# One attention-and-feed-forward kernel: the denominator of the last batch by another route, and a new written order of work

## The chip, the cores and the metric

The kernel runs on one core of one Trainium2 chip. The metric is the device time of one execution in microseconds (us); lower is better. The core has five engines that this text names by their short names in the profile: PE (TensorE, the matrix engine; PEld is its weight load), DVE (VectorE), ACT (ScalarE), POOL (GpSimd) and SP (SyncE, which here only issues DMAs). SBUF is the on-chip working memory, PSUM the memory into which PE writes and from which DVE and ACT read.

## The reference

Four batches of four heads, 1088 positions, 32 features a head, in float32. Each query and key is projected to 8 numbers by S1 and to 8 by S2, and the 64 pairwise products are its features. Attention is linear in them; its output, 128 numbers a position, goes through a feed-forward layer of width 2048.

```python
def phi(x):
    a = np.einsum('rd,bhsd->bhsr', S1, x)
    b = np.einsum('rd,bhsd->bhsr', S2, x)
    return np.einsum('bhsi,bhsj->bhsij', a, b).reshape(*x.shape[:-1], r * r)
q_p, k_p = (phi(q), phi(k))
kv = np.einsum('bhsf,bhsd->bhfd', k_p, v)
z = np.sum(k_p, axis=2)
num = np.einsum('bhsf,bhfd->bhsd', q_p, kv)
den = np.einsum('bhsf,bhf->bhs', q_p, z)[..., None] + 1e-06
return (num / den).astype(np.float32)
...
h = x @ w_in
g = h * (1.0 / (1.0 + np.exp(-beta * h)))
return (g @ w_out).astype(np.float32)
```

## The kernel before, in words

**Two jobs woven together.** The feed-forward part is cut into 68 waves of 1024 columns of hidden values. The step `f17a`, `f17b` (function `first`, L725) is two matmuls of 512 columns that fill a two-bank PSUM tile `wave` for wave 17; one ACT instruction (L734, SiLU) then reads the whole tile into `gT`; `s17a`, `s17b` (function `second`, L757, or L749 for the last two chunks) multiply it by the output weights into `acc`. There are two `wave` tiles, so a new `f` needs the ACT instruction of the wave two before it. Eight waves make a chunk of 512 positions; the last three chunks have 256 positions and four waves each. Positions are packed over batches: 34 units of 32 positions a batch. Chunk 5 (waves 40 to 47) still needs batch 2 alone; chunk 6, from wave 48, is the first that needs batch 3.

**The attention steps of a batch b** (the batch is the last digit of a step's name): `kta`, `ktb`, `qt` transpose the loaded rows on DVE; `kpj`, `qpj` project on PE; `ktn`, `qtn` turn the result back on DVE; `kp0` to `kp3` form the key features (`k_product`, L372, on POOL or DVE); `kv0` to `kv3` sum features times v on PE (L520); `kvo` and three small DMAs `kr` spread that sum. The denominator takes a route of its own: `zs` (L393) lets PE sum products of the projections into z, `zc` copies it out, `wp` (L407) folds S2 into it, `wm` masks it, `cpj` (L450) multiplies the transposed queries by it, `ctn` turns the result, `c`, on DVE (L461). Then `dp` (L473) multiplies the first query projection with c, `ds` sums, `dr` takes the reciprocal (L490), `an` scales the projection by it (L496). `qp` forms the scaled query features (L372), `qpt` transposes them, `num` (L571) multiplies them with the spread sum on PE, and `xa`, `xb`, `xc` (`x_copy`, L601) copy the result to `xall`, in half precision, from where the waves read it. Batch 0 does its query side in two parts; the first has an `x` in its names.

**Copies of the last batch.** The last two chunks (16 units) leave the kernel in another layout, and `x_copy` writes those units of batch 3 in an interleaved order. So each of `xa3`, `xb3`, `xc3` is two instructions.

**What sets the order.** Nothing is scheduled automatically: `ORDER` is one list of step names, written out, and every engine's queue is that list filtered to its own instructions. Each engine runs its queue strictly in order, so one late step holds all behind it. `ENGINES` says on which engine the movable steps run. `i5` in the list is five matmuls on zeros that nobody reads (L340). SP issues all loads in the list's order too: `lk`, `lq`, `lv` for keys, queries and values, `li`, `lba`, `lo` for the weights, which `wb` (L310) and `wo` (L313) rescale. `wb0` and `wo0` serve waves 0 and 1, `wb1` and `wo1` waves 2 and 3, and so on. Keys and queries of batches 1 to 3 share one buffer, so `lk20` waits until `kta1` and `ktb1` have read batch 1.

```python
KC = ((0, 2), (2, 4), (4, 6), (6, 9))
XPARTS = (("x", (0, 4)), ("", (4, NC)))
...
for name in ORDER.split():
    if name[0] == "i" and name[1:].isdigit():
        idle(int(name[1:]))
    else:
        ops.pop(name)()
```

Of the kernel before, what the change touches and what calls it, by code (L numbers as in the profile page):

```python
# [12 lines left out]
P = 128  # L13
# [4 lines left out]
def kernel(  # L18
# [34 lines left out]
    lk0a ls2 lk0b lq0a ident pads warm i3 lv02 li0 lv00 ls1 lb i4 zms tbl lv01 sp kta0 masks ktb0 i2 sbd lv03  # L53
    qt0x0 kpj0 ktn0 sel kp10 sp2 kp30 bt i2 s2s lk11 lba1 li2 kp20 bc i3 kp00 zs0 lk10 zc0 qpjx0 wp0 wm0 i1 i2
    lba0 qtnx0 cpjx0 kv00 rb i5 ctnx0 kv30 kv10 kv20 kvw0 kvt0 dpx0 lo0 dsx0 drx0 anx0 qp00 lq0b li1 i7 kvc0 lo1
    qp10 qpt10 qpt00 lba3 lba2 ktb1 numx0 qt00 lq11 cpj0 lq10 xcx0 kta1 li3 qpj0 wb0 wo0 wb1 xax0 xbx0 wo1 i1
    f0a f0b ctn0 f1a qtn0 lo2 wb2 f1b lk21 dp0 lk20 ds0 kpj1 dr0 an0 f2a qp30 f2b s0a qp20 f3a f3b lv11 s0b s1a
    lo3 qt01 s1b s2a s2b lv13 qpt30 ktn1 qt11 wb3 f4a f4b f5a s3a qpt20 wo2 s3b f5b zs1 qpj1 qtn1 lv10 f6a zc1
    s4a wp1 wm1 f6b kp01 s4b wo3 num0 xb0 xc0 kta2 cpj1 xa0 lq20 f7a lq21 lv12 f7b kp21 s5a f8a kp31 s5b f8b
    ktb2 s6a ctn1 s6b s7a f9a kp11 f9b s7b lk30 f10a f10b kpj2 kv31 kv21 kv11 kv01 dp1 lk31 ds1 dr1 f11a f11b  # L60
    an1 qp21 o0 f12a s8a qt02 kvo1 f12b kr21 s8b kr31 ktn2 qp01 s9a s9b qpt21 qpt01 s10a f13a f13b s10b s11a
    qp11 qpt11 kr11 qt12 s11b f14a kp02 s12a f14b s12b f15a s13a lv23 s13b ktb3 f15b zs2 num1 zc2 lv21 s14a xc1
    s14b lq31 xa1 xb1 kp32 s15a lv20 lv22 s15b f16a f16b f17a kta3 wp2 f17b qpj2 wm2 cpj2 f18a f18b kp22 kp12
    qtn2 ctn2 f19a dp2 f19b lq30 kpj3 kv12 kv22 f20a o1 ds2 f20b dr2 s16a an2 f21a f21b kv02 qp02 kv32 f22a f22b
    s16b s17a f23a kvo2 f23b s17b s18a qpt02 s18b f24a f24b s19a kr22 s19b f25a qp12 f25b s20a s20b s21a lv30
    f26a f26b kr32 ktn3 qpt12 qp22 s21b s22a f27a f27b s22b s23a qpt22 s23b f28a f28b lv32 kr12 zs3 num2 zc3 xb2
    o2 wp3 xa2 f29a f29b xc2 lv31 s24a s24b kp33 f30a lv33 f30b s25a kp03 s25b qt13 s26a wm3 s26b f31a qt03 f31b
    s27a f32a f32b cpj3 qpj3 f33a f33b f34a s27b s28a f34b s28b s29a s29b f35a kp23 f35b s30a ctn3 s30b f36a
    qtn3 kp13 f36b dp3 ds3 s31a kv23 dr3 kv13 f37a f37b s31b o3 f38a an3 f38b kv03 qp13 kv33 f39a f39b kvo3 s32a
    s32b qp23 f40a kr23 f40b s33a s33b s34a f41a f41b kr13 qp03 s34b s35a f42a f42b s35b s36a s36b f43a kr33  # L70
    f43b s37a s37b qpt03 f44a f44b s38a qpt13 qpt23 s38b s39a f45a f45b s39b num3 xb3 o4 f46a f46b s40a xa3 xc3
    f47a f47b s40b s41a s41b f48a f48b s42a s42b f49a f49b s43a s43b f50a f50b s44a s44b s45a f51a f51b s45b
    s46a f52a f52b s46b s47a s47b f53a f53b f54a o5 f54b s48a s48b s49a f55a f55b s49b s50a f56a f56b s50b s51a
    f57a f57b s51b s52a s52b f58a f58b s53a s53b f59a f59b s54a s54b s55a s55b f60a f60b f61a o6 f61b s56a s56b
    s57a s57b f62a f62b s58a s58b f63a f63b s59a s59b o7 s60a f64a f64b s60b s61a f65a f65b s61b s62a s62b f66a
    f66b s63a s63b o8 f67a f67b s64a s64b s65a s65b s66a s66b s67a s67b o9
# [3 lines left out]
        "kp10": "p", "kp30": "p", "kp20": "p", "kp00": "v", "zc0": "a", "kvw0": "a", "qp00": "p", "kvc0": "a",  # L80
        "qp10": "v", "xcx0": "a", "wb0": "p", "wo0": "p", "wb1": "p", "xax0": "a", "xbx0": "a", "wo1": "p",
        "wb2": "p", "qp30": "v", "qp20": "p", "wb3": "p", "wo2": "p", "zc1": "a", "kp01": "p", "wo3": "p",
        "xb0": "a", "xc0": "a", "xa0": "a", "kp21": "p", "kp31": "p", "kp11": "p", "qp21": "p", "qp01": "p",
        "qp11": "p", "kp02": "p", "zc2": "a", "xc1": "v", "xa1": "a", "xb1": "a", "kp32": "p", "kp22": "p",
        "kp12": "v", "qp02": "v", "qp12": "v", "qp22": "p", "zc3": "v", "xb2": "a", "xa2": "v", "xc2": "v",
        "kp33": "p", "kp03": "p", "kp23": "v", "kp13": "v", "qp13": "p", "qp23": "p", "qp03": "v", "xb3": "a",
        "xa3": "v", "xc3": "v",
# [370 lines left out]
    def c_turn(b, c0, c1):  # L458
        if "tcc" not in st[b]:
            st[b]["tcc"] = sb.tile([P, G, R], F32, tag="tcc", name="tcc")  # L460
        nc.vector.transpose(  # L461
            out=ap(st[b]["tcc"], c0 * T, [[1, (c1 - c0) * T]]),
            in_=ap(c_at(b, c0), c0 * T, [[1, (c1 - c0) * T]]),
        )
# [6 lines left out]
    def den_product(b, c0, c1):  # L471
        g0, n = 4 * c0, 4 * (c1 - c0)
        nc.vector.tensor_tensor(  # L473
            out=prods[b % 2][:, g0 : g0 + n, 0:R],
            in0=ap(st[b]["tq"], g0 * 2 * R, [[2 * R, n], [1, R]]),
            in1=st[b]["tcc"][:, g0 : g0 + n, :],
            op=ALU.mult,
        )
# [8 lines left out]
    def den_turn_over(b, c0, c1):  # L487
        own(b, "rden", [P, G])
        g0, n = 4 * c0, 4 * (c1 - c0)
        nc.vector.reciprocal(out=st[b]["rden"][:, g0 : g0 + n], in_=st[b]["den"][:, g0 : g0 + n])  # L490

    def a_scale(b, c0, c1):
        own(b, "an", [P, G, R])
        g0, n = 4 * c0, 4 * (c1 - c0)
        a = ap(st[b]["tq"], g0 * 2 * R, [[2 * R, n], [1, R]])
        nc.vector.tensor_tensor(  # L496
            out=st[b]["an"][:, g0 : g0 + n, :], in0=a, in1=ap(st[b]["rden"], g0, [[1, n], [0, R]]), op=ALU.mult
        )
# [14 lines left out]
    def kv_sum(b, cs):  # L513
        kp = st[b]["kp"]
        t = kv_at(b)
        for c in cs:
            n = P if c < NC - 1 else 64
            done = st[b].setdefault("kvn", 0)
            for h in range(H):
                nc.tensor.matmul(  # L520
                    out=t[T * h : T * h + T, :],
                    lhsT=v_in[b][:n, h, c, :],
                    rhs=kp[:n, 4 * c + h, :],
                    start=(done == 0),
                    stop=(done == NC - 1),
                    skip_group_check=True,
                )
            st[b]["kvn"] += 1

# [49 lines left out]

    TURNED = 16  # L580

    def x_copy(b, j, c0, c1, eng):

        js, tile = ((0, 1), 0) if j < 0 else ((j,), j)
        n = min(c1, (U - js[0] + 3) // 4) - c0
        cut = n
        if b == B - 1:
            cut = min(n, (U - TURNED - js[0] + 3) // 4 - c0)
            assert all((U - TURNED - x + 3) // 4 - c0 == cut for x in js)
        for k0, k1 in ((0, cut), (cut, n)):  # L590
            if k0 == k1:
                continue
            u = 4 * (c0 + k0) + js[0]
            step_j, step_t = T, 1
            at = b * S + u * T
            if k0 == cut and b == B - 1:
                v = u - (U - TURNED)
                step_j, step_t = 1, 4
                at = b * S + (U - TURNED) * T + v // 4 * P + v % 4
                assert v % 4 + len(js) <= 4  # L600
            eng(  # L601
                out=ap(xall, at, [[step_j, len(js)], [P, k1 - k0], [step_t, T]]),
                in_=ap(st[b]["xp", c0][tile], k0 * T, [[512, len(js)], [T, k1 - k0], [1, T]]),
            )

    KC = ((0, 2), (2, 4), (4, 6), (6, 9))
    XPARTS = (("x", (0, 4)), ("", (4, NC)))
    for b in range(B):
# [4 lines left out]
        step(f"zs{b}", z_sum, b)  # L613
        step(f"zc{b}", lambda b=b: z_copy(b, cop(f"zc{b}")))
        step(f"wp{b}", w_project, b)
        step(f"wm{b}", w_mask, b)
# [13 lines left out]
        for x, us, (c0, c1) in parts:  # L630
            for i, (u0, u1) in enumerate(zip(us, us[1:])):
                step(f"qt{i}{x}{b}", q_transpose, b, u0, u1)
            step(f"qpj{x}{b}", q_project, b, c0, c1)
            step(f"qtn{x}{b}", q_turn, b, c0, c1)
            step(f"cpj{x}{b}", c_project, b, c0, c1)
            step(f"ctn{x}{b}", c_turn, b, c0, c1)
            step(f"dp{x}{b}", den_product, b, c0, c1)
            step(f"ds{x}{b}", den_sum, b, c0, c1)
            step(f"dr{x}{b}", den_turn_over, b, c0, c1)
            step(f"an{x}{b}", a_scale, b, c0, c1)  # L640
# [18 lines left out]
    assert u == B * U and TURNED == sum(n for _, n in chunks[-2:])  # L659
# [10 lines left out]
    turned = (LAST - 1, LAST)  # L670

# [43 lines left out]
    def first(s, w):  # L715
# [7 lines left out]
        for i in range(half):  # L723
# [4 lines left out]
                rhs=xall[:, u0 * T : u0 * T + n],  # L728
# [79 lines left out]
```

## Time and profile before

| | us |
|---|---|
| Median of 3 runs (lowest, highest) | 103.58 (103.08, 103.79) |
| The profiled execution, its own time | 103.39 |
| Its span, first to last instruction | 101.6 |
| Around the span | 1.8 |
| First wave matmul on PE (`f0a`) starts | 17.96 |
| `num3`, the last attention matmuls, start and next wave matmul | 72.95 and 74.45 |
| Last matmul ends | 97.74 |

| us busy of the span | PE | DVE | ACT | POOL |
|---|---|---|---|---|
| 0 to 18 | 16.2 | 11.1 | 4.0 | 12.0 |
| 18 to 72 | 53.9 | 43.3 | 44.8 | 28.6 |
| 72 to 96 | 23.2 | 4.6 | 22.3 | 0 |

Times in the profile are counted from the first instruction. A matmul's busy time overlaps that of its neighbours, since they are pipelined; what one costs PE is the distance from its start to the next one's start, and that is what is used below. The granted clock of TensorE was 1.00 over the span.

### The profile page before, as it was taken

What the parts mean: (1) busy time and instruction counts of PE and PEld (TensorE: products, weight loads), DVE (VectorE), ACT (ScalarE), POOL (GpSimd) and SP (SyncE); (2) the same over time, 40 slices, a digit from 0 to 9 for tenths busy, and PEclk for the clock granted to TensorE, in tenths of its full rate; (3) what the DMA queues carried; (4) which work ended last, traced back from release to release, by engine and by line L of the source; (5) the groups of instructions that cost most, each with busy time, mean ns of one, the idle gap of its engine ahead of it and who ended that gap; (6) DMA issues with size and microseconds to landing.
All of it is one profiled execution on the core that took longest, in us unless ns stands there. A gap on an engine that the chain in (4) does not pass through costs nothing.

```text
span 101.6 us, 3172 instructions
## 1 busy us (share of the span) xinstructions
PE 94.9 (93%) x1342; PEld 48.2 (47%) x1342; DVE 59.3 (58%) x111; ACT 72.5 (71%) x93; POOL 40.6 (40%) x49
## 2 busy tenths in 40 slices
PE   5999989999999999999999999999979999999940
PEld 1244554344436454344436434544424436689930
DVE  1564888999798994798953967389342020021110
ACT  1412022687795984789995779899967999989930
POOL 6409599999997993008090000085000000000000
PEclk9999999999999999999999999999999999999999
DMA  2999999983661545614320064052003205013411
GB/s 43 326 285 315 388 354 404 328 250 84 238 219 31 91 99 161 215 25 76 83 74 13 10 100 110 0 87 55 0 13 60 37 11 92 0 19 67 74 54 52
DMA packets 24253, 12.56 MB, mean 124 GB/s; under 512 B 17024, under 2 KB 21936, under 8 KB 24240
## 3 DMA queue, kind: packets, MB, share of 16 engines
q1 hardware_dynamic: 24032, 12.29, 43.8%
q8 instruction: 10, 0.16, 0.7%
q10 hardware_dynamic: 208, 0.08, 0.3%
q14 instruction: 3, 0.02, 0.1%
HBM read 9.84 MB, written 2.23 MB: 119 GB/s over the span
## 4 chain that ended last, share of the span: by engine, by line
PE 86%; ACT 8%; DVE 1%; issue 1%; DVEq 0%; ACTq 0%
PE wave L725 27%; PE acc L757 23%; PE idle L340 9%; ACT gT L734 7%; PE at L520 6%; PE xp L571 5%; PE fin L749 4%; PE qpp L430 3%; PE at L450 2%; PE kpp L357 2%; PE at L393 2%; PE xw L571 1%; PE at L548 1%; ACT xall L601 1%; PE at L407 1%
## 5 line engine op out<-in xcount | busy, mean ns | idle before, releaser
L734 ACT ACTIVATE gT<-wave 128x1024 f16<-128x1024 f32 (+1 forms) x69 | 65.8, 1011 | 8.3 <-PE wave L725 7.8
L725 PE MATMUL wave<-xall,winb 128*128 128x512 f16 (+1 forms) x160 | 40.8, 347 | 1.0 <-DVE xall L601 0.7
L757 PE MATMUL acc<-gT,woutp 128*128 128x512 f16 (+1 forms) x128 | 34.7, 366 | 0.0
L372 POOL TENSOR_TENSOR qp<-an,tq 128x768 f32<-128x768 f32 (+1 forms) x8 | 13.9, 1759 | 22.1 <-DVE an L496 22.1
L725 PEld LDWEIGHTS <-winb 128*128 128x128 f16 x160 | 14.7, 99 | 16.7 <-issue 3.8
L757 PEld LDWEIGHTS <-woutp 128*128 128x128 f16 x128 | 12.4, 97 | 12.8 <-issue 0.4
L372 POOL TENSOR_TENSOR kp<-tk 128x512 f32<-128x512 f32 (+1 forms) x12 | 15.0, 1274 | 6.3 <-DVE tk L368 6.3
L684 DVE STREAM_TRANSPOSE osb<-acc 128x512 f32<-128x512 f32 (+1 forms) x8 | 5.4, 680 | 18.0 <-PE acc L757 15.1
L508 DVE STREAM_TRANSPOSE qpt<-qp 128x768 f32<-128x768 f32 (+1 forms) x13 | 11.1, 883 | 0.3 <-POOL qp L372 0.2
L340 PE MATMUL idle<-warm 128*128 128x512 f16 x30 | 9.6, 454 | 1.3 <-DVE tiny L231 1.3
L344 DVE STREAM_TRANSPOSE kT<-k_in 128x576 f32<-128x576 f32 (+1 forms) x8 | 5.6, 715 | 2.4 <-DMA k_in<-in_k_dram 2.4
L571 PE MATMUL xp<-qpt,kvr 32*32 32x288 f32 (+2 forms) x160 | 6.9, 364 | 0.0
L571 PE MATMUL xw<-qpt,kvr 32*32 32x256 f32 (+1 forms) x160 | 6.8, 343 | 0.0
L520 PE MATMUL at<-kp,v_in 128*32 128x64 f32 (+1 forms) x288 | 6.3, 223 | 0.0
L520 PEld LDWEIGHTS at<-kp,v_in 128*32 128x32 f32 (+1 forms) x288 | 4.7, 109 | 3.2 <-issue 1.7
L349 DVE STREAM_TRANSPOSE qT<-q_in 128x512 f32<-128x512 f32 (+1 forms) x8 | 5.7, 718 | 0.3 <-DMA q_in<-in_q_dram 0.3
L310 POOL TENSOR_TENSOR winb<-w_in_sb,beta_all 128x512 f16<-128x512 f32 x4 | 5.2, 1292 | 0.0
L340 PEld LDWEIGHTS <-warm 128*128 128x128 f16 x30 | 2.9, 111 | 4.5 <-issue 1.6
L601 ACT CAST xall<-xw 128x128 f16<-128x128 f32 (+1 forms) x9 | 2.6, 327 | 3.0 <-PE xw L571 2.0
L571 PEld LDWEIGHTS xp<-qpt,kvr 32*32 32x32 f32 x160 | 3.7, 103 | 2.3 <-issue 0.8
L372 DVE TENSOR_TENSOR qp<-an,tq 128x768 f32<-128x768 f32 (+1 forms) x5 | 4.5, 905 | 0.1
L749 PE MATMUL fin<-woutp,gT 128*128 128x128 f16 x64 | 4.4, 219 | 0.0
(74 smaller groups left out, 71.1 us busy)
## 6 DMA issues: line engine op xcount, KB each, us to landing
k_in<-in_k_dram SPq DMA_DIRECT2D x6, 272.0 KB, 4.6
q_in<-in_q_dram SPq DMA_DIRECT2D x6, 272.0 KB, 4.0
v_in<-in_v_dram SPq DMA_DIRECT2D x8, 144.0 KB, 3.6
v_in<-in_v_dram SPq DMA_DIRECT2D x8, 128.0 KB, 3.3
w_in_sb<-in_moe_w_in_dram SPq DMA_DIRECT2D x4, 256.0 KB, 5.1
beta_all<-in_moe_beta_dram SPq DMA_DIRECT2D x4, 256.0 KB, 6.0
w_out_sb<-in_moe_w_out_dram SPq DMA_DIRECT2D x4, 256.0 KB, 5.3
out_dram<-osb SPq DMA_DIRECT2D x16, 64.0 KB, 1.9
```

The source lines that it names most:

```text
L340: nc.tensor.matmul(out=t[:, 0, :], lhsT=warm[:, 0:P], rhs=warm, start=True, stop=True)
L344: nc.vector.transpose(out=kT[:, u0:u1, :].rearrange("p u t -> p (u t)"), in_=k_in[b][:, u0 * D : u1 * D])
L349: nc.vector.transpose(out=qT[:, u0:u1, :].rearrange("p u t -> p (u t)"), in_=q_in[b][:, u0 * D : u1 * D])
L372: eng.tensor_tensor(out=ap(o, g0 * F, [[F, n], [R, R], [1, R]]), in0=ap(a, g0 * a_step + a_off, [[a_step, n], [1, R], [0, R]]), in1=ap(bsr ...
L508: nc.vector.transpose(out=ap(st[b]["qpt"], c0 * H * F, [[1, (c1 - c0) * H * F]]), in_=ap(st[b]["qp"], c0 * H * F, [[1, (c1 - c0) * H * F]]),)
L520: nc.tensor.matmul(out=t[T * h : T * h + T, :], lhsT=v_in[b][:n, h, c, :], rhs=kp[:n, 4 * c + h, :], start=(done == 0), stop=(done == NC - 1),
L571: nc.tensor.matmul(out=ts[j][T * h : T * h + T, 0 : n * T], lhsT=st[b]["kvr"][p : p + T, f, h, :], rhs=ap(st[b]["qpt"], (4 * c0 + h) * F + ...
L684: nc.vector.transpose(out=osb[:, :un, :].rearrange("p u m -> p (u m)"), in_=accs[ci][:, : un * T])
L725: nc.tensor.matmul(out=wvs[s][:, w, i * n : i * n + n], lhsT=winb[:, j * P : j * P + P], rhs=xall[:, u0 * T : u0 * T + n], start=True, sto ...
L734: nc.scalar.activation(out=g[:, o + i * 512 : o + i * 512 + 1024 // m], in_=wvs[s].rearrange("p a n -> p (a n)")[:, i * 512 : i * 512 + 10 ...
L749: nc.tensor.matmul(out=accs[ci][a][:, 0:DM], lhsT=gts[s // GP][:, o + a * P : o + a * P + P], rhs=woutp[:, j, :], start=(j == 0), stop=(j ...
L757: nc.tensor.matmul(out=accs[ci][:, :n], lhsT=woutp[:, j, :], rhs=gts[s // GP][:, o : o + n], start=(j == 0), stop=(j == NJ - 1),)
```

## The change

Four things change in the code, and with them the whole written order.

**1. Batch 3 takes a new route to c.** `zs3`, `zc3`, `wp3`, `wm3`, `cpj3` and `ctn3` go. In their place five adds `su03` to `su43` fold the key features over the nine position blocks (DVE: `su03`, `su23`, `su33`; POOL: `su13`, `su43`). `zm3` multiplies the folded features by a 128x128 matrix of ones on PE, so that every partition gets z; `zy3` copies it to SBUF (DVE). Three products `bz03`, `bz23` and `bz13` of second query projection and z (POOL, DVE, POOL; 768 elements each) and three DVE sums `br03`, `br13`, `br23` give c. Batches 0 to 2 keep the old route.

**2. Plain copies.** `x_copy` writes batch 3 as the other batches, one instruction for each of `xa3`, `xb3`, `xc3`. A new DVE step `xr` later copies the last 512 columns of `xall` in the interleaved order to `xlast`, which the last two chunks read.

**3. PSUM for batch 0's first part.** Its c (`ctnx0`) and reciprocal (`drx0`) are written to PSUM, in the bank `cb`, and not to SBUF.

**4. Engines.** `dp` and `an` may now run on POOL: `dp0`, `dp1`, `dp2`, `dp3`, `an0`, `an2` do. Of the weights, `wb3` and `wo3` move from POOL to DVE. `xa2` and `xc2` move from DVE to ACT; in batch 3, `xa3` is now on ACT and `xb3` on DVE. Key and query products are dealt out anew (`kp33` to DVE and `kp13`, `kp23` to POOL, for one).

```diff
+    def k_add(b, eng, i):
...
+        o, x, y = {
+            0: (ks[:, 0:2], k(0, 2), k(4, 2)),
+            1: (ks[:, 2:4], k(2, 2), k(6, 2)),
+            2: (ks[:, 0:2], ks[:, 0:2], ks[:, 2:4]),
+            3: (ks[:, 0:1], ks[:, 0:1], ks[:, 1:2]),
+            4: (ks[0:64, 0:1], ks[0:64, 0:1], k(8, 1, 64)),
+        }[i]
...
+        eng.tensor_tensor(out=w(o), in0=w(x), in1=w(y), op=ALU.add)
+
+    def z_wide(b):
+        nc.tensor.matmul(out=bank(b)[:, 0 : H * F], lhsT=ones, rhs=st[b]["ks"][:, 0, :], start=True, stop=True)
...
+    def c_product(b, eng, c0, c1):
...
+            out=ap(st[b]["bz"], 4 * c0 * F, [[H * F, n], [F, H], [R, R], [1, R]]),
+            in0=ap(st[b]["tq"], 4 * c0 * 2 * R + R, [[H * 2 * R, n], [2 * R, H], [0, R], [1, R]]),
+            in1=ap(st[b]["zw"], 0, [[0, n], [F, H], [R, R], [1, R]]),
+            op=ALU.mult,
...
+    def c_sum(b, c0, c1):
...
+        nc.vector.reduce_sum(
...
+    def c_turned(b, c0, c1):
+        if b == 0 and c0 == 0:
+            return cb[:, 256 : 256 + c1 * T].rearrange("p (g r) -> p g r", r=R)
...
+    def rden_at(b, c0, c1):
+        if b == 0 and c0 == 0:
+            return cb[:, 384 : 384 + 4 * c1]
...
-        for k0, k1 in ((0, cut), (cut, n)):
...
+    def x_last():
+        nc.vector.tensor_copy(
+            out=xlast.rearrange("p (a t i) -> p a t i", i=4, t=T), in_=ap(xall, LAST0, [[P, NLAST // P], [1, T], [T, 4]])
+        )
...
-                rhs=xall[:, u0 * T : u0 * T + n],
+                rhs=xlast[:, u0 * T - LAST0 :][:, :n] if ci in turned else xall[:, u0 * T : u0 * T + n],
```

**The order that follows.** PE's queue up to the first wave, before and after:

```
before: i3 i4 sp i2 kpj0 sp2 bt i2 i3 zs0 qpjx0 wp0 i1 i2 cpjx0 kv00 i5 kv30 kv10 kv20 kvt0 i7 numx0 cpj0 qpj0 i1 f0a
after:  i6 i2 sp i1 kpj0 sp2 bt i3 i2 zs0 qpjx0 wp0 i2 cpjx0 qpj0 i2 i2 i2 kv10 kv00 kv30 kv20 kvt0 i3 cpj0 numx0 i2 f0a
```

DVE's queue after, for batch 3 and the end: `ktn3 qp12 qpt02 qpt22 qpt12 kp33 su03 qt13 qt03 su23 su33 o2 qtn3 zy3 bz23 kvo3 br23 br03 br13 o3 ds3 dr3 an3 qp13 qpt13 qpt03 qpt23 o4 xb3 xc3 o5 xr o6`. POOL's: `qp22 kp13 kp23 kp03 su13 su43 bz03 bz13 dp3 qp03 qp23`. Stores `o` wait for PE's sums of a whole chunk. On PE `zm3` stands behind `f30b`, and `num3` behind `f45b`, as before. On SP the second half of the weights is now interleaved with later loads: `lk20` comes ahead of `lba3`, `li3`, `lo2` and `lo3`.

## The prediction

> **What bounds the kernel now.** I read the page's busy times first, then a table of busy times by stretches of the span, the chain of waits in order of time, and the timeline where the chain leaves PE.
>
> ```profile
> PE 94.9 (93%) x1342; PEld 48.2 (47%) x1342; DVE 59.3 (58%) x111; ACT 72.5 (71%) x93; POOL 40.6 (40%) x49
> ...
> PE 86%; ACT 8%; DVE 1%; issue 1%; DVEq 0%; ACTq 0%
> ```
>
> ```profile
> 66.00:72.00 6.00, 6.00 (x51) 2.75 (x40) 5.16 (x9) 5.92 (x8) 3.69 (x2) 1.00 0.32 60
> 72.00:78.00 6.00, 5.25 (x82) 2.25 (x81) 2.30 (x5) 4.63 (x7) 0.00 (x0) 1.00 0.13 21
> ```
>
> After the stretch stand its length and the busy time of PE, PEld, DVE, ACT and POOL. PE is busy without a hole from the first wave at 17.96 us to its last matmul at 97.74, but for 0.75 us in the second row. A busy row proves little for a pipelined engine, so I also took starts: back-to-back 512-column matmuls start 0.216 us apart all along (70.27, 70.70, 71.13 for pairs). The starts show three excesses: 0.27 us at 20.09, 0.91 at 74.89, 0.26 at 82.10. So PE's queue is the bound: what leaves it after 17.96 is gained, unless a wait takes its place. ACT is next, 22.3 of the 24 us from 72 to 96. The large excess is this:
>
> ```profile
> 74.45 0.60 PE L725 MATMUL wave<-xall,winb 128*128 128x512 f16 x2
> 74.89 0.38 PE L757 MATMUL acc<-gT,woutp 128*128 128x512 f16 x1
> 75.09 1.02 ACT L734 ACTIVATE gT<-wave 128x1024 f16<-128x1024 f32 x1
> 75.23 0.64 DVE L601 CAST xall<-xw 128x128 f16<-128x128 f32 x2 [1.46 <-ACT xall L601]
> 75.68 1.14 DVE L601 CAST xall<-xp 128x320 f16<-128x320 f32 x2
> 76.02 0.59 PE L725 MATMUL wave<-xall,winb 128*128 128x512 f16 x2 [0.75 <-DVE xall L601]
> ```
>
> `num3` took a `wave` tile as output; `f47` at 76.02 needs it back, after two ACT copies (74.59 to 75.20) and two DVE copies that wait for ACT's.
>
> **PE's own work.** The steps removed, start to next start:
>
> ```profile
> 53.32 0.61 PE L393 MATMUL at<-tk 128*32 128x16 f32 x36
> ...
> 55.37 0.40 PE L407 MATMUL at<-zs,s2sel 128*128 128x16 f32 x2
> 55.61 0.59 PE L725 MATMUL wave<-xall,winb 128*128 128x512 f16 x2
> ...
> 58.94 0.69 PE L450 MATMUL at<-qT,wz 128*32 128x288 f32 x8
> 59.56 0.71 PE L430 MATMUL qpp<-qT,sbd 64*32 64x288 f32 x16
> ```
>
> `zs3` 0.54, `wp3` 0.24, `cpj3` 0.62: 1.40. Added is `zm3`, 128x256 in f32, which no row shows. `kvt0`, two 128x128 f32 matmuls, took 0.55 (13.64 to 14.19); with half of that hidden it would be 0.27, twice that 1.1. I take 0.55, the same columns. Each change from half precision to f32 costs 0.09 more (0.31 for 0.22 before such groups). After the first wave there are 15 such groups before and 16 after: 0.09. Net: -1.40 + 0.55 + 0.09 = **-0.76**.
>
> **Up to the first wave: 0.** `f0a` waits for `xbx0`, that for `numx0`. The side that makes `qpt00` gets shorter: `dpx0` took 0.83 beside a POOL product, the 128-element `anx0` took 0.29 with POOL idle. With c in PSUM I take 0.35 (bounds 0.29 and 0.83), and `wm0`, which reads PSUM and SBUF beside POOL, took 0.19. But `qtn0` (0.52) now stands ahead of `qpt10`, so `qpt00` still ends near 15.1. On PE six idle matmuls (1.42) and `qpj0` (0.44) precede all the `kv` (1.75 to `kvt0`): `cpjx0` near 9.95, `kv` from 12.2, `kvt0` 14.3, `kvc0` until 15.4, `i3` until 15.55, `cpj0` (0.50), `numx0` at 16.05. Before it was 15.79. Then `i2` (0.47) runs while ACT copies until 17.85, and `f0a` comes near 17.95. `wb0` is now second behind `wb1` on POOL: 13.7 + 2 x 1.27 = 16.25, in time. If that cover goes, each microsecond is a microsecond. Bounds: -0.4 (`cpj0` and the idle matmuls overlap the copies) to +0.4.
>
> **From there to `num3`: +0.25.** A step costs nothing where it is ready before PE reaches it. I added up PE's rows in the new order and walked DVE's and POOL's queues beside it. One mechanism rules the walk:
>
> ```profile
> 26.68 3.77 POOL L372 TENSOR_TENSOR kp<-tk 128x512 f32<-128x512 f32 x3
> ...
> 27.99 1.54 DVE L473 TENSOR_TENSOR prod<-tq,tcc 128x288 f32<-128x288 f32 x1
> ...
> 61.66 0.45 DVE L473 TENSOR_TENSOR prod<-tq,tcc 128x288 f32<-128x288 f32 x1
> ```
>
> The same `dp` takes 0.45 alone and 1.54 when a POOL product of 1.51 runs: the later one waits for the earlier. So I let DVE's and POOL's two-input operations exclude each other. The Trainium skill, "SBUF — State Buffer", section "Who interferes with whom", states this as an exclusive lock on a port pair, for a VectorE instruction with two SBUF inputs against a GpSimd one that reads SBUF. By it `bz23`, `bz03` and `bz13` run one after another, 3.9 us; if they only shared, they would take 3.0 and `num3`'s spare time below would be 0.9 more; the end would not move. The trace agrees with the lock (1.54 against 0.45).
>
> Early: `wo0` ends at 19.0 for `s0a` at 20.0; `ktn1` 20.75 for `qpj1` at 20.95; `wb3` by 24 for `f6` at 24.6. `wo2` and `wb3` wait for loads that `lk20` holds until `kta1` is done (17.85); loads of 256 KB landed in 2.8 to 3.6 us at the start, and in about 5 with many in flight. I take 3: `lo2` 22.5.
>
> Last batch: `ktn3` ends at 48.8. POOL's `kp13`, `kp23`, `kp03` end at 52.9, `kp33` 53.7, `su03` 54.4, `su13` 55.35 (1.07, a 512-element POOL product), `su23` and `su33` 56.9, `su43` 57.5. PE is at `zm3` at 58.3 with the delays so far: 0.8 to spare. Then `zm3` 58.9, `zy3` 59.4, `bz23` 60.4 (0.95), `bz03` 61.8, `bz13` 63.3, `br13` 64.25. The reductions are 0.9 each: 0.30 for 144 inputs and 0.48 for 324 give 1 ns an input. Then `dp3` 65.0 on POOL (0.68), and DVE is held by `o3` until 65.6, which waits for `s31b`. `ds3`, `dr3`, `an3` 66.95, `qp13` 67.9, `qp03` 69.3, `qp23` 70.8, `qpt23` 71.75. PE reaches `num3` near 72.3: 0.5 to spare.
>
> The +0.25 is ACT. All of batch 2's copies are on ACT now (`xc2`, 576 elements, about 0.6 by its rows of 0.37 for 256 and 0.43 for 320), and from `f38` to `f45` the new order has a wave every 0.89 us where the old one had 1.01. ACT needs 0.90 to 0.95 a wave. Bounds 0 and 0.7.
>
> **After `num3`: -0.75.** `num3` to the last matmul is 23.29 now, 0.91 of it the stall. The chain to a free tile is now `xa3` (ACT, 0.37), then `xb3` (DVE, 0.42), since DVE's copy waited for ACT's here: 1.05 to 1.1 with hand-overs. Ahead of `f47` stand `f46` and two halves of `s40`, 0.87. The stall left is 0.2, a gain of 0.7. ACT sets the pace behind it, 0.26 now; the new order gives PE more `s` ahead of `f54`, but meets `f60` with less, so I keep 0.2. `xr` (512 elements, near 0.7) lies on an idle DVE at about 80, six microseconds ahead of `f60`.
>
> **Sum.** 0 - 0.76 + 0.25 - 0.75 = -1.26, on the profiled execution 103.39 - 1.26 = 102.13. That execution lies 0.19 under the median, so the time forecast is 103.58 - 1.26 = **102.3**.
>
> **Rivals.**
> - *More comes off (0.17).* ACT's pace costs nothing, and the side towards `f0a` gains its 0.4: -1.9, 101.7; with `zm3` at 0.27, 101.4. For it: `dpx0`'s 0.5. Against: PE's queue ahead of `numx0` is full.
> - *Weights come late (0.15).* `lba3`, `li3`, `lo2` stand behind `lk20`, and land in 5 to 6 us, the page's medians for them: `wb3` ends at 25.1 and `wo2` at 25.8, for `f6` and `s4` at 24.85 and 25.3 (with drift). PE stalls 0.8 to 1.0: 103.2. Against it: DMA traffic falls from 300 GB/s to 84 by 23 us.
> - *The last batch's chain is late (0.18): slower.* No row prices the adds, the `bz` products and their sums. If they are half as dear again as I took (`qp03`-like POOL products do take 2.2 where they wait), the `su` steps end 1.35 later, 0.65 beyond what `zm3` spares, and the rest 2.4 later, of which `o3` and `num3`'s spare time hide 1.1: a stall of 1.95 in all, -1.26 + 1.95 = +0.7, 104.3. It decides once `num3`'s operands come 0.5 us late, and the time passes 103.58 at 1.8. Against: the product's row is close kin.
>
> **How the numbers follow.** The forecast has 0.50, with a range of its own of 101.7 to 102.9 (the bounds above). About 1% is what a measurement tells here, so faster is under 102.54 and slower over 104.6. Of the forecast's 0.50 some 0.35 lies under 102.54; with the first rival, faster is 0.52. Slower is the last rival's worse part (half as dear again gives 104.3, more than that passes 104.6) and what I have not seen: 0.15. Same is the remaining 0.15 of the forecast, the weights' 0.15 and 0.03 of the last: 0.33. For eight in ten the range reaches over the first rival's 101.4 and into the last one's, to 104.0.
>
> **What would show it.** PE: no rows of batch 3 at the lines of `zs`, `wp`, `cpj`; `zm3` near 0.55; `f0a` near 17.95; `num3` near 72.4 and next wave 1.5 later; 0.2 before `f47`. If `f6` or `s4` waits for POOL or DVE, the weights were late; if `zm3` or `num3` waits for POOL or DVE, the chain was. The forecast is wrong if the first wave comes after 18.5, or PE's starts show more than 1 us of new excess before `num3`.

## The result, and the profile after

| | before | after |
|---|---|---|
| Median, us (lowest, highest, runs) | 103.79 (103.08, 106.02, 5) | 107.22 (106.46, 107.93, 5) |
| Ratio after to before, 95% interval | | 1.0361 (1.0315 to 1.0407) |
| The profiled execution, its own time | 103.39 | 106.46 |

The change makes the kernel 3.6% slower; the forecast was 102.3 us, 1.2% faster. Some executions of nearly every kernel here are 2 to 4% longer than the rest of the same kernel; medians include them, the ratios leave them out, and where a profile is of such a long execution the text says so.

The two profiled executions, cut at marks on PE, show where 3.07 us came from. The last column belongs to an experiment below, the same changed kernel with another order of loads; its profiled execution is the fastest of six.

| us | before | after | difference | forecast | `e5_sp` |
|---|---|---|---|---|---|
| up to `f0a` | 17.96 | 19.47 | +1.51 | 0 | 17.40 (-0.56) |
| `f0a` to `num3` | 54.99 | 57.68 | +2.69 | -0.51 | 55.19 (+0.20) |
| `num3` to the last matmul's start | 24.57 | 23.87 | -0.70 | -0.75 | 23.86 (-0.71) |
| from there to the end of the execution's time | 5.87 | 5.44 | -0.43 | 0 | 5.42 (-0.45) |
| sum | | | +3.07 | -1.26 | -1.52 |

So all of the loss lies before `num3`. The page of the changed kernel:

```profile
PE 97.4 (93%) x1295; PEld 48.9 (47%) x1295; DVE 60.9 (58%) x109; ACT 72.9 (70%) x94; POOL 48.7 (47%) x57
...
GB/s 62 323 253 275 303 375 286 18 254 279 301 189 10 137 130 120 253 153 6 100 177 74 9 18 25 82 0 110 15 0 31 75 0 100 0 20 74 36 75 51
...
PE 63%; ACT 13%; DMA 9%; DVE 8%; SPq 2%; issue 1%; ACTq 0%
```

PE's busy share is what it was (93%) and says nothing of the loss. The last row, the chain of waits, says where to look: DMA (9%) and SP's queue (2%) are in it, where before neither was. But its shares don't measure the loss either: in the faster `e5_sp` they are as large (PE 63%, DMA 11%, SP's queue 6%). PE's starts, below, do. In the GB/s row (40 slices of 2.6 us) the eighth slice, 18.3 to 20.9 us, moves 18 GB/s between neighbours of 286 and 254: in the middle of the loads, the DMA engines had almost nothing to do. The table of busy times by stretches (columns as in the prediction) shows where PE paid; the kernel before comes first, then the changed one:

```profile
24.00:30.00 6.00, 6.00 (x111) 2.71 (x104) 5.08 (x8) 4.53 (x9) 6.00 (x6) 1.00 0.64 208
30.00:36.00 6.00, 6.00 (x107) 2.95 (x106) 5.42 (x12) 4.66 (x5) 5.35 (x5) 1.00 0.30 55
36.00:42.00 6.00, 6.00 (x133) 2.88 (x131) 4.30 (x8) 3.90 (x8) 3.07 (x3) 1.00 0.58 158
```

```profile
24.00:30.00 6.00, 5.38 (x68) 2.16 (x71) 4.14 (x7) 3.54 (x5) 3.60 (x4) 1.00 1.06 289
30.00:36.00 6.00, 5.62 (x135) 2.84 (x132) 4.81 (x12) 3.69 (x7) 4.94 (x4) 1.00 0.41 100
36.00:42.00 6.00, 5.46 (x74) 2.62 (x88) 4.67 (x7) 4.50 (x6) 5.45 (x5) 1.00 0.54 118
...
78.00:84.00 6.00, 6.00 (x57) 2.59 (x51) 1.09 (x2) 5.25 (x7) 0.00 (x0) 1.00 0.27 47
```

From 24 to 42 us PE has 1.54 us of holes, where before it had none; the hole of 0.75 us after `num3` is gone. The list of waits (who waited for whom; us in total, times, longest) names what PE's helpers, and PE itself, waited for:

```profile
POOL woutp L316 <- DMA w_out_sb<-in_moe_w_out_dram: 4.0, 1, 4.0
DVE kT L347 <- DMA k_in<-in_k_dram: 3.9, 3, 2.4
...
DVE winb L313 <- DMA w_in_sb<-in_moe_w_in_dram: 1.8, 1, 1.8
...
PEld xp L632 <- DMA kvr<-kvr: 1.1, 1, 1.1
...
PE xp L632 <- DMA kvr<-kvr: 0.5, 1, 0.5
```

They are four load-bound places: `wo2` (its load `lo2`), `wb3` (`li3`), `ktb2` (`lk21`; the longest of that row's three waits, 2.4, is for batch 0's first load and is there in `e5_sp` too), and `num1` itself, which waits for the `kr` copies of its spread sum. PE's rows at these places:

```profile
26.37 0.60 PE L797 MATMUL wave<-xall,winb 128*128 128x512 f16 x2
27.50 0.39 PE L829 MATMUL acc<-gT,woutp 128*128 128x512 f16 x1 [0.52 <-POOL woutp L316]
...
32.98 0.72 PE L360 MATMUL kpp<-kT,sbd 64*32 64x288 f32 x16 [0.38 <-DVE kT L347]
...
41.56 0.67 PE L632 MATMUL xp<-qpt,kvr 32*32 32x288 f32 x2 [0.54 <-DMA kvr<-kvr]
```

Beyond the usual distance from start to start (0.22 us, 0.31 before a group in f32, 1.50 for the whole of `num1`) PE loses 0.26 us before `f6` (26.37, for `wb3`), 0.68 before `s4a` (27.50, for `wo2`), 0.45 before `kpj2` (32.98) and 1.43 inside `num1`: 2.82 in all. PE's queue in `e5_sp` is the same, so the two can be laid side by side: from `f0a` to the last matmul their starts drift apart at these four places, and by 0.35 us the other way at 20.24, where `e5_sp` waits for a query load; after `num1` they don't part any more. So the new route, the new copies and ACT's pace, which both kernels share, have no part in the loss.

SP's part of the timeline (start, duration, issue) shows the root:

```profile
14.75 0.43 SPq L189 DMA_DIRECT2D w_in_sb<-in_moe_w_in_dram  x1
19.48 0.48 SPq L176 DMA_DIRECT2D k_in<-in_k_dram  x1
20.00 0.59 SPq L217 DMA_DIRECT2D beta_all<-in_moe_beta_dram  x1
20.63 0.43 SPq L189 DMA_DIRECT2D w_in_sb<-in_moe_w_in_dram  x1
21.10 0.43 SPq L192 DMA_DIRECT2D w_out_sb<-in_moe_w_out_dram  x1
...
24.12 0.48 SPq L176 DMA_DIRECT2D k_in<-in_k_dram  x1
```

and the same kernel's list of SP's waits:

```profile
SPq L176 <- DVE den L497: 4.4, 1, 4.4
```

After `li2` at 14.75, SP issues nothing until 19.48: the next in its queue is `lk20`, which may not overwrite batch 1's keys before DVE has transposed them (`kta1`; the row names DVE's last instruction before SP went on). SP waits 4.4 us, and behind it stand `lba3`, `li3` and `lo2`, whose buffers are free, and `lk21`. The Trainium skill, "DMA: Bandwidth & Descriptors", section "Anatomy of one DMA — SWDGE (gpsimd) path", has it that DMA engines don't wait on semaphores: the wait takes place on the issuing sequencer ahead of dispatch. That section is on DMAs issued by GpSimd; these are issued by SP, and the hole agrees. What was issued after the hole went out in one bunch: `lk21` took 7.0 us to land (24.12 to 31.13). The late issue is what counts: in `e5_sp` `lk21` takes 7.9 us, but is issued 6.2 us sooner (17.93). In the kernel before, SP had issued all weights but `lo3` ahead of the two loads of batch 2's keys that wait (the last row):

```profile
14.55 0.34 SPq L186 DMA_DIRECT2D w_in_sb<-in_moe_w_in_dram  x1
15.27 0.38 SPq L189 DMA_DIRECT2D w_out_sb<-in_moe_w_out_dram  x1
17.09 1.12 SPq L173 DMA_DIRECT2D k_in<-in_k_dram  x2
```

### The profile page after: what moved, and what is told of

It reads as the page before. It is cut to its first block, busy times and chain, and to the rows that moved or that the text cites. A ratio compares the mean times of both kernels' runs of the same rounds, so it can differ in the third digit from the quotient of the medians.

```text
span 104.7 us, 3087 instructions
## 1 busy us (share of the span) xinstructions
PE 97.4 (93%) x1295; PEld 48.9 (47%) x1295; DVE 60.9 (58%) x109; ACT 72.9 (70%) x94; POOL 48.7 (47%) x57
## 4 chain that ended last, share of the span: by engine, by line
PE 63%; ACT 13%; DMA 9%; DVE 8%; SPq 2%; issue 1%; ACTq 0%
PE wave L797 19%; PE acc L829 13%; ACT gT L806 12%; PE idle L343 8%; DMA k_in<-in_k_dram 7%; PE at L534 5%; PE xp L632 4%; PE fin L821 3%; DMA kvr<-kvr 2%; PE kpp L360 2%; PE qpp L433 2%; DVE qpt L522 2%; DVE tk L371 2%; DVE kT L347 1%; SPq L179 1%; PE xw L632 1%
## 5 line engine op out<-in xcount | busy, mean ns | idle before, releaser
L797 PE MATMUL wave<-xall,winb 128*128 128x512 f16 (+1 forms) x128 | 35.8, 366 | 0.5 <-ACT xall L649 0.2
L375 POOL TENSOR_TENSOR kp<-tk 128x512 f32<-128x512 f32 (+1 forms) x14 | 17.0, 1235 | 5.4 <-DVE tk L371 5.4
L375 POOL TENSOR_TENSOR qp<-an,tq 128x768 f32<-128x768 f32 (+1 forms) x6 | 11.3, 1896 | 4.4 <-DVE an L510 4.3
L632 PE MATMUL xp<-qpt,kvr 32*32 32x288 f32 (+2 forms) x160 | 7.8, 364 | 0.5 <-DMA kvr<-kvr 0.5
L347 DVE STREAM_TRANSPOSE kT<-k_in 128x512 f32<-128x512 f32 (+1 forms) x8 | 5.7, 727 | 3.9 <-DMA k_in<-in_k_dram 3.9
L375 DVE TENSOR_TENSOR qp<-an,tq 128x768 f32<-128x768 f32 (+1 forms) x7 | 6.4, 924 | 0.3 <-POOL an L510 0.2
L487 POOL TENSOR_TENSOR prod<-tq,tcc 128x288 f32<-128x288 f32 (+1 forms) x4 | 3.4, 840 | 6.8 <-DVE tcc L475 5.7
L574 POOL TENSOR_TENSOR bz<-tq,zw 128x768 f32<-128x768 f32 x2 | 4.3, 2195 | 2.6 <-DVE zw L568 2.6
L649 ACT CAST xall<-xw 128x256 f16<-128x256 f32 (+1 forms) x9 | 2.7, 331 | 3.6 <-PE xp L632 2.0
```

The lines of the kernel that those rows point to most:

```text
L347: nc.vector.transpose(out=kT[:, u0:u1, :].rearrange("p u t -> p (u t)"), in_=k_in[b][:, u0 * D : u1 * D])
L375: eng.tensor_tensor(out=ap(o, g0 * F, [[F, n], [R, R], [1, R]]), in0=ap(a, g0 * a_step + a_off, [[a_step, n], [1, R], [0, R]]), in1=ap(bsr ...
L574: eng.tensor_tensor(out=ap(st[b]["bz"], 4 * c0 * F, [[H * F, n], [F, H], [R, R], [1, R]]), in0=ap(st[b]["tq"], 4 * c0 * 2 * R + R, [[H * 2 ...
L632: nc.tensor.matmul(out=ts[j][T * h : T * h + T, 0 : n * T], lhsT=st[b]["kvr"][p : p + T, f, h, :], rhs=ap(st[b]["qpt"], (4 * c0 + h) * F + ...
L797: nc.tensor.matmul(out=wvs[s][:, w, i * n : i * n + n], lhsT=winb[:, j * P : j * P + P], rhs=xlast[:, u0 * T - LAST0 :][:, :n] if ci in tu ...
```

## The experiments

The theory: the loss is all in the order of SP's queue, at three places: (1) weights behind the waiting `lk20`, (2) `kr` of batch 1 behind `lv22`, `lv21` and late k loads, (3) the first part's v, `lv02`, eleventh of all loads where it was fourth. Rivals: PE's idle matmuls (6+2+1 where there were 7+2) let its clock rise late; the new route or the new copies cost more than thought. SP's queue in short, changed part by part (`...` the rest as it was):

```
before: lk0a lk0b lq0a lv02 li0 lv00 lv01 lv03 ... lo1 lba3 lba2 lq11 lq10 li3 lo2 lk21 lk20 lv11 ... lk30 lk31 o0 kr21 kr31 kr11 lv23 lv21 ...
after:  lk0b lk0a lq0a lq0b lv01 lv00 lo0 lba0 lv03 li1 lv02 ... lba2 li2 lk20 lba3 li3 lo2 lq21 lo3 lv11 lv13 lk21 ... lk31 o0 lv22 lv21 kr31 kr11 kr21 lv20 lk30 ...
```

**The weights first: `e1_loads`** (place 1 alone)

```diff
-... lba2 li2 lk20 lba3 li3 lo2 lq21 lo3 lv11 ...
+... lba2 li2 lba3 li3 lo2 lo3 lk20 lq21 lv11 ...
```

> The changed kernel, with the loads lba3, li3, lo2 and lo3 put ahead of lk20 in SP's queue; nothing else. Theory A (a load that waits, put ahead of weights, empties the DMA queues and bunches what follows): the waits before f6 and s4a (0.95 us in the changed kernel's profile) go, and most of the 0.45 us before f10a; wo2's load lands before 23 us; time 105.3 to 105.9 against 107.2 for the change. Theory B (the loads are late because there are too many of them, whatever the order): the DMA queues stay full and the same waits turn up at other steps, 107.0 to 107.4. Both leave the wait before num1 (1.4 us) largely alone.

Measured: 105.78 us (105.57 to 106.79, 4 runs), ratio 1.0223 (1.0155 to 1.0290). The waits before `s4a` and `kpj2` are gone, that at `num1` stays (1.63 us beyond its usual length), and the first `kv` group starts 1.15 us late. A hole of 0.9 us inside `zs1`, at 22.7, is new; the profile shows no releaser for it, and its cause is open. Place 1 is real, 1.4% by the two ratios (0.5 and 0.7% either way), and not all.

**And `kr` ahead of the v loads: `e2_loads_kr`** (places 1 and 2)

```diff
-... lk31 o0 lv22 lv21 kr31 kr11 kr21 lv20 lk30 ...
+... lk31 o0 kr31 kr11 kr21 lv22 lv21 lv20 lk30 ...
```

> As e1_loads, and lv22, lv21 put behind the three kr copies of batch 1 in SP's queue. Theory A: num1 no longer waits for the spread sum, another 1.0 to 1.4 us: 104.0 to 104.8. Theory B: unchanged from e1_loads.

Measured: 106.04 us, but 102.81 to 107.68 in 4 runs, too scattered for a ratio. In its profile, a long execution, `num1` waits for nothing. In exchange `lk30`, issued at 39.62, lands at 43.7; `kta3` waits for it on DVE, `wm2` stands behind `kta3`, and PE stands still 2.27 us for `wm2`. Freeing one place moved the wait to the next load in line.

**`kr` and both k loads, weights still late: `e8_kr`**

```diff
-... lk31 o0 lv22 lv21 kr31 kr11 kr21 lv20 lk30 ...
+... lk31 lk30 o0 kr31 kr11 kr21 lv22 lv21 lv20 ...
```

> The changed kernel with two moves in SP's queue alone: lk30 next to lk31, and the kr copies of batch 1 ahead of lv22, lv21. The weights stay behind lk20 and v of batch 0 stays late. Theory A: num1's wait (1.3 to 1.4 us in the profiles of the change, e1_loads, e3_idle) falls under 0.3 and no wait like e2_loads_kr's 2.5 us before cpj2 follows; the waits before s4a and f10a stay, about 1.4 us. 105.4 to 106.2. Theory E (waits only move on): num1 or the next attention step still waits over 1 us, and the time is the change's, 106.5 to 107.9.

Measured: 106.60 us (106.14 to 108.14, 4 runs), ratio 1.0278 (1.0214 to 1.0342). The wait at `num1` did not go (1.71 us); on this point the expectation fell. SP's timeline of this kernel:

```profile
32.39 1.12 SPq L176 DMA_DIRECT2D k_in<-in_k_dram  x2
33.60 2.61 SPq L762 DMA_DIRECT2D out_dram<-osb  x4
36.31 2.27 SPq L599 DMA_DIRECT2D kvr<-kvr  x3
```

`lk31` and `lk30` wait for `ktb2`, that for the late `lk21`: so 544 KB and four stores go out right ahead of the small `kr` copies. The hole at 15 to 19 us is paid again at 40. That they stand ahead of `kr` isn't the whole cause: in `e5_sp` below the same loads and stores do. There the k loads are issued at 29.25 and not at 32.39, and the last copy lands 1.88 us after its issue, here 3.60.

**All three but the v order: `e9_kr_loads`** (`e8_kr` with `lba3 li3 lo2 lo3` ahead of `lk20`)

> e8_kr with lba3, li3, lo2, lo3 ahead of lk20 too: all of e5_sp's moves but the early v of batch 0 (and the order of lv, lq behind). Theory A: only the first kv group's wait for v (about 1.1 us, first wave near 18.5 and not 17.4) and a wait of up to 1 us before f4 are left: 103.6 to 104.6.

Measured: 103.84 us (103.08 to 106.24, 10 runs), ratio 0.9983 (0.9943 to 1.0023). `num1` no longer waits. What is left is a hole of 0.63 us inside `zs1`, as open as that in `e1_loads`, and place 3, seen in PE's timeline:

```profile
11.02 1.47 PE L343 MATMUL idle<-warm 128*128 128x512 f16 x6
13.97 1.12 PE L534 MATMUL at<-kp,v_in 128*32 128x64 f32 x56 [1.48 <-DMA k_in<-in_k_dram]
```

The row names a k load, which `kv` doesn't read. The v load `lv02`, issued at 6.85, landed at 13.72, 0.25 us ahead of this row; it is the operand that was missing. In `e1_loads`, `e2_loads_kr`, `e3_idle` and `e8_kr` too the group starts 0.24 or 0.25 us after `lv02` lands.

**All three: `e5_sp`**, the changed kernel in everything but SP's queue:

```diff
-lk0b lk0a lq0a lq0b lv01 lv00 lo0 lba0 lv03 li1 lv02 lba1 lk10 lk11 li0 lo1 lq11 lq10 lba2 li2 lk20 lba3 li3 lo2 lq21 lo3 lv11 lv13 lk21 lv12 lv10 lq20 lk31 o0 lv22 lv21 kr31 kr11 kr21 lv20 lk30 lv23 ...
+lk0b lk0a lq0a lq0b lv02 lv00 lv01 lv03 lo0 lba0 li1 lba1 lk11 lk10 li0 lo1 lba2 li2 lq11 lq10 lba3 li3 lo2 lo3 lk20 lk21 lv11 lv13 lv12 lv10 lq20 lq21 lk31 lk30 o0 kr21 kr31 kr11 lv22 lv21 lv20 lv23 ...
```

> The changed kernel with another order of loads in SP's queue alone: v of batch 0 ahead of the weights, all weights ahead of lk20, lk30 next to lk31, the kr copies of batch 1 ahead of batch 2's v. Every other queue is as in the change. Theory A (SP's order of loads is the cause): no wait over 0.3 us at the first kv group, before s4a, f10a, num1 or cpj2; first wave near 17.9, num3 near 72.7; 102.1 to 102.7, below the kernel before. Theory E (the changed orders of PE, DVE and POOL cost the time themselves): waits turn up at the same steps behind DVE or POOL, 104.5 or more.

Measured: ratio 0.9883 (0.9823 to 0.9942); median 103.22 us (101.87 to 105.76, 6 runs), beside 103.75 before. The order of loads alone turns the changed kernel from 3.6% slower to 1.2% faster than before by the ratio; by the medians the gain is 0.5%, so not every execution has it. Place 3 is the least well shown: from `e9_kr_loads` to here lie 1.0%, with intervals that just don't touch, other v and q loads moved as well, and it was not put into the kernel before by itself. For it speaks that `f0a` comes at 17.21 to 17.40 us in the three profiles with `lv02` fifth (this one, `e6_oldroute`, `e12_xc2`), and at 17.87 to 19.48 in the six with it eleventh. SP's timeline of this kernel:

```profile
15.34 1.03 SPq L192 DMA_DIRECT2D w_out_sb<-in_moe_w_out_dram  x2
17.41 1.13 SPq L176 DMA_DIRECT2D k_in<-in_k_dram  x2
...
29.25 1.11 SPq L176 DMA_DIRECT2D k_in<-in_k_dram  x2
30.46 2.52 SPq L762 DMA_DIRECT2D out_dram<-osb  x4
33.08 2.27 SPq L599 DMA_DIRECT2D kvr<-kvr  x3
```

`lk20` waits here too, but with the weights already under way; `kr` is issued at 33.08, 5.2 us sooner than in the changed kernel (38.25), and is in SBUF when `num1` comes.

**The orders put into the kernel before: `e7_spswap`, `e10_before_lk`, `e11_before_kr`.** The first takes the whole SP queue of the changed kernel (but for one late `kr` copy behind `o3`), the others one place each:

```diff
-... lo1 lba3 lba2 lq11 lq10 li3 lo2 lk21 lk20 lv11 ...
+... lo1 lk21 lk20 lba3 lba2 lq11 lq10 li3 lo2 lv11 ...
```

```diff
-... o0 kr21 kr31 kr11 lv23 lv21 lq31 ...
+... o0 lv23 lv21 kr21 kr31 kr11 lq31 ...
```

> The kernel before with the changed kernel's order of loads in SP's queue; nothing else (PE, DVE, POOL and ACT as before, old route, old copies). Theory A: it becomes slower by most of what the change lost, 105 to 106.5, with waits for loads before the early s and f steps and before num1. Theory E: 103.4 to 104.

> The kernel before with lk21 and lk20 moved ahead of lba3, lba2, lq11, lq10, li3, lo2 in SP's queue; nothing else. Theory A: those six loads wait until kta1 has read the buffer (17.1 us) and land 4 us or more later; wb2 and f4 wait, 1 to 2.5 us more than the kernel before: 104.6 to 106.2. Theory E: 103.4 to 104.

> The kernel before with lv23 and lv21 moved ahead of the kr copies of batch 1 in SP's queue; nothing else. The copies are issued 1.2 us later; num1 started within 0.1 us of their landing. Theory A: 0.8 to 1.3 more, 104.4 to 104.9. If num1 has more time than I think: 103.6.

Measured: `e7_spswap` 115.26 us, ratio 1.1003 (1.0930 to 1.1076): it costs this kernel far more than the 105 to 106.5 us expected; in its profile, a long execution, the first `kv` group alone waits 3.6 us. That kernel was written around other loads. `e10_before_lk` 109.13 us, ratio 1.0546 (1.0487 to 1.0605), more than expected. Its waits and its stretch from 25 to 28 us:

```profile
POOL winb L310 <- DMA beta_all<-in_moe_beta_dram: 5.7, 2, 5.6
...
PE wave L725 <- POOL winb L310: 3.5, 1, 3.5
```

```profile
25.00:28.00 3.00, 2.63 (x6) 0.74 (x6) 2.42 (x4) 1.02 (x1) 2.97 (x3) 0.52 1.12 283
```

PE waits 3.5 us for a weight tile, and then runs for some 3 us at half rate (granted clock 0.52), which costs another 1.5 us. `e11_before_kr` 104.44 us, ratio 1.0080 (1.0045 to 1.0115): two v loads of 128 to 144 KB ahead of `kr` make `num1` wait in a kernel where it never did:

```profile
PEld xp L571 <- DMA kvr<-kvr: 1.1, 1, 1.1
...
PE xp L571 <- DMA kvr<-kvr: 0.5, 1, 0.5
```

Places 1 and 2 are thus shown from both sides: with the rest of the kernel new (`e1_loads`, `e9_kr_loads`), and with the rest old. Either by itself keeps the wait at `num1`: it stays in `e1_loads` and in `e8_kr`.

**The idle matmuls: `e3_idle`**

```diff
-i6 ... i1 kpj0
+i5 ... i2 kpj0
```

(the changed kernel with the split of before, 7 and 2 with those around)

> The changed kernel with the idle matmuls ahead of sp and kpj0 as before the change (7 and 2 in place of 8 and 1); nothing else. Theory C (the arrangement of the idle matmuls decides at which window PE leaves its slow phase, 0.45 against 0.236 us for 512 columns): the slow phase ends near 6.5 us, not near 10, the first wave starts near 18.0 and not 19.5, 105.7. Theory D (where that window falls is chance, whatever the kernel): the first wave starts at either, and the times are those of the change, 106.5 to 107.9, with the same spread.

Measured: 106.25 us (105.96 to 106.89, 4 runs), ratio 1.0257 (1.0199 to 1.0315). In its profile `f0a` comes 1.60 us sooner, at 17.87, but the whole execution is only 0.50 shorter (105.96 against 106.46): `kpj2` now waits 1.07 us beyond the usual distance and `num1` 1.83, since PE reaches the same late loads sooner. By the ratios the kernel is 1.0% faster than the changed one, with intervals that touch. A good part of the 1.51 us up to `f0a` in the first table only covered the late loads.

**The new copies alone: `e4_plain`** (the kernel before with the plain `xa3`, `xb3`, `xc3` and `xr` ahead of `f59b`)

```diff
-... s53b f59a f59b ...
+... s53b f59a xr f59b ...
```

> The kernel before with only the second part of the change: one copy each for xa3, xb3, xc3, and xr (ahead of f59b on DVE). If the copies were the cause of the 0.91 us before f47: that wait falls to 0.3 and the time to 103.0 (0.5 to 0.7 less). If xr or something else takes it back: 103.6.

Measured: ratio 0.9929 (0.9901 to 0.9956), 0.73 us of 103.53; forecast for this part 0.75. In its profile (a long execution) the two halves around the old hole start 0.58 us apart:

```profile
77.70 0.38 PE L756 MATMUL acc<-gT,woutp 128*128 128x512 f16 x1
78.28 0.59 PE L724 MATMUL wave<-xall,winb 128*128 128x512 f16 x2 [0.20 <-DVE xall L589]
```

where it was 1.13 us before, and 0.22 would be no hole.

**The old route to c: `e6_oldroute`** (`e5_sp` with `zs3 zc3 wp3 wm3 cpj3 ctn3` in place of `su03` to `su43`, `zm3`, `zy3`, `bz` and `br`)

```diff
-    WIDE = (3,)
+    WIDE = ()
```

> As e5_sp, but batch 3 takes the old route to c too (zs3, zc3, wp3, wm3, cpj3, ctn3 in place of the adds, the ones matmul, the three products and sums). If PE's work sets the time, as forecast, 0.7 to 0.9 more than e5_sp. If the new route buys nothing, since its products hold DVE and POOL: the same as e5_sp, or less.

Measured: ratio 1.0015 (0.9966 to 1.0063), 104.86 us in 12 runs. Between the two lie 1.3%, some 0.8 either way; the forecast for the route was 0.76 us, 0.7%. That it gains in this order is shown, its size isn't: the order was written for the new route, and the old steps were put into its places. In the profile, a long execution, the stretch from `num1` to `num3` is 1.55 us longer than in `e5_sp` (35.41 against 33.86). Some 0.9 of it are the old steps themselves; the rest are two short holes that another placement might not have.

**ScalarE's pace: `e12_xc2`** (`e5_sp`, with `xc2` on DVE)

```diff
-"xc2": "a"
+"xc2": "v"
```

> This is e5_sp with one thing changed: the plain copy of x of batch 2's last heads (xc2) is made on VectorE instead of ScalarE. It tests the term 'ScalarE's pace before f38 to f39, +0.25', which measured 0.39 us of excess in e5_sp. Theory (the excess is ScalarE's pace): the excess before f38/f39 falls to 0.1 or less, and the time is 0.2 to 0.4 us below e5_sp (ratio to before 0.984 to 0.987 where e5_sp had 0.9883). Rival (VectorE has no room there: its copy pushes su33, su43 and with them zm3's chain later, or makes the wave wait for VectorE's den): the excess stays or moves to another wave, and the time is that of e5_sp within 0.2 us or up to 0.5 us above (ratio 0.988 to 0.993). The loads are e5_sp's, so the kr waits should stay absent and f0a should end near 17.4.

Measured: ratio 0.9845 (0.9781 to 0.9909), not to be told from `e5_sp`. Its profile (a long execution) answers the question for that place: the excess before `f38` and `f39` is 0.41 us in both kernels, and the next five waves add 0.28 more in both, 0.69 in all. So `xc2` has no part in it. ACT is busy without a hole there (3.00 of 3 us, 64 to 67 in `e5_sp`), and the waves themselves are left as its cause, which is argued: no run tried to change them. The same profile shows that even this order is near the edge; beside 0.7 us before `f6`, `num1` takes 1.73 us more than usual:

```profile
39.63 0.43 PE L632 MATMUL xp<-qpt,kvr 32*32 32x288 f32 x1 [1.01 <-DMA kvr<-kvr]
```

The third `kr` copy, issued at 35.63, landed at 39.59 here, 4.0 us after its issue; in `e5_sp` one issued at 34.76 landed at 36.64. Why one execution differs so from another is open.

## Why the prediction was wrong

**The steps that failed** are two. *"From there to `num3`: +0.25"* came out at +3.20 (2.69 against -0.51 with PE's own work, which lies in that stretch). The walk went down DVE's, POOL's and PE's queues, but of SP's it priced only `lo2` and `wb3`, with "I take 3" for their landing. `lo2` was issued at 21.10 and not 19.5, since `lk20` was free at 19.48 and not at 17.85, and it landed 5.3 us later: `wo2` got it at 26.4, not at 22.5. Loads that took 6.6 us stood in the profile before (`lo1` to `lq10`). `lk21` and the `kr` copies, which the new order moved as well, were never walked. The rival *"Weights come late"* named the mechanism and the landing of 5 to 6 us, but ended at `wb3` and `wo2`, with 0.8 to 1.0; `wb3` and `wo2` cost PE 0.94 (0.26 and 0.68), but what stands behind them in SP's queue went on: `kpj2` (0.45), which is gone once the weights are in time (`e1_loads`), and `num1` (1.43), whose wait goes only where weights and `kr` are both moved (`e2_loads_kr`, `e9_kr_loads`, `e5_sp`). The evidence cited against it, DMA traffic falling to 84 GB/s by 23 us, was the old order's, and the wait for `lk20` is what changed that.

*"Up to the first wave: 0"* came out at +1.51. On the engines nothing was lost: with the v loads first, `f0a` comes at 17.40 (`e5_sp`), which is even more than the bound of -0.4. But the step never asked when `lv02` lands, which had gone from fourth to eleventh: the `kv` group starts 1.15 us late for it in `e1_loads` and 1.55 in `e9_kr_loads`. In the changed kernel's own profile PE's slow start (below) covers that wait.

**The steps that held.** *After `num3`: -0.75* measured -0.70 in the changed kernel and -0.71 in `e5_sp`. PE's starts at the old hole in the changed kernel:

```profile
78.65 0.60 PE L797 MATMUL wave<-xall,winb 128*128 128x512 f16 x2
79.09 0.59 PE L829 MATMUL acc<-gT,woutp 128*128 128x512 f16 x2
79.67 0.59 PE L797 MATMUL wave<-xall,winb 128*128 128x512 f16 x2
```

Two halves of 0.215 from 79.09 would end at 79.52; the stall left is 0.15, where 0.2 was forecast. *PE's own work: -0.76* took 0.55 for `zm3`; it is 0.44, from its start to the next in `e5_sp`. The step as a whole came out smaller, since other f32 groups got longer in the new order: all of them together are 0.58 us shorter. `zm3`:

```profile
58.01 0.60 PE L563 MATMUL at<-ks,ones 128*128 128x256 f32 x2
58.45 0.38 PE L797 MATMUL wave<-xall,winb 128*128 128x512 f16 x1
```

*The last batch's chain* held against the rival that would have made it late, as DVE's rows of `e5_sp` show:

```profile
58.65 0.42 DVE L568 COPY zw<-at 128x256 f32<-128x256 f32 x1 [0.48 <-PE at L563]
...
63.51 0.95 DVE L585 TENSOR_REDUCE tcc<-bz 128x96 f32<-128x768 f32 x1 [0.80 <-POOL bz L574]
...
70.62 0.98 DVE L522 STREAM_TRANSPOSE qpt<-qp 128x768 f32<-128x768 f32 x1 [0.49 <-POOL qp L375]
```

Against the forecast: `zm3` 58.01 (58.3), `bz23` until 60.07 (60.4), `bz13` until 63.48 (63.3), `br13` until 64.46 (64.25), `an3` until 66.76 (66.95), `qpt23` until 71.60 (71.75), `num3` 72.59 (72.3). These are times from the start, and `f0a` came 0.55 sooner than forecast, so the stretch from `f0a` to `num3` is longer by 0.8. *`dpx0` 0.35* is 0.29, below.

**A size that was off, and luck.** *ACT's pace: +0.25* measured up to 0.69 (`e5_sp` and the changed kernel alike; see `e12_xc2`). The sum, -1.26, is near what `e5_sp` measures as a ratio (-1.2% of 103.75 is 1.2 us), as if the forecast had been that of a kernel whose loads come in time. In part that is luck. From `f0a` to `num3` its profile has +0.20 and not -0.51: ACT's pace cost 0.4 more, the wait for a query load 0.35, and PE's own work gained 0.2 less; the other way, a hole of 0.27 that the kernel before had at 20.09 is gone. Two gains make up for it: 0.56 up to `f0a`, beyond the bound of -0.4, and 0.45 behind the last matmul's start, where nothing was forecast. The latter is in every profile of the new order (5.4 us) and in none of the old (5.8 to 6.0, with the plain copies too); its cause is open.

## What to carry to other kernels

A change that rewrites an order has to be walked on the queue that issues the loads as on the engines: for each load, what it waits for, what stands behind it, and how long a bunch takes to land. A load that waits for its buffer holds all loads behind it, and the delay comes back later, with the loads that wait for the readers of the late ones; so put what waits for nothing ahead of what does, and small copies on the critical path ahead of big loads. And a landing time of an idle moment is not that of a bunch (3 us against 5 to 8 here): price it with the row of the crowded stretch.

## What the runs showed of the hardware

**PE at half rate.** At the start the matmuls of 512 columns lie 0.43 us apart, later 0.22. The switch comes early or late with nothing changed that explains it. The same five idle matmuls, in the changed kernel and in `e3_idle`:

```profile
7.66 2.31 PE L343 MATMUL idle<-warm 128*128 128x512 f16 x5
```

```profile
6.62 1.25 PE L343 MATMUL idle<-warm 128*128 128x512 f16 x5
```

In `e4_plain`, with the idle matmuls of before, the slow phase lasted to 9.9 us too; in `e1_loads`, with those of the changed kernel, it had ended by 7.2; in `e10_before_lk`, by 4.6. So their arrangement doesn't decide it. The granted clock reads 1.00 in both phases. The Trainium skill, "TensorE: Matmul & The Clock Gate", section "Part 1: The HAM clock gate", has half rate as the default, full rate after a busy window of about 3.4 us, and a window that runs freely, so that the moment differs from run to run. The earliest case agrees (PE's first matmul at 1.25, full rate by 4.6); the latest, 8.6 us after the first matmul, is more than two such windows. Half rate also follows a wait: after 3.5 us in `e10_before_lk` (clock 0.52, above), and after 2.3 us in `e2_loads_kr`, where the next 3 us have a granted clock of 0.52.

**A product that reads PSUM does not wait for POOL.** `dpx0` beside a POOL product, in `e1_loads`:

```profile
9.37 2.53 POOL L375 TENSOR_TENSOR kp<-tk 128x768 f32<-128x768 f32 x2
...
10.92 0.29 DVE L487 TENSOR_TENSOR prod<-tq,cb 128x128 f32<-128x128 f32 x1
```

It took 0.29 us, here and beside such a product in seven other profiles of the new code; with both operands in SBUF it had taken 0.83 beside such a product, and 0.29 without one (`e4_plain`, where POOL is idle at that moment).
